# Running gate/up of all units, then down of all, in the last two passes of a two-layer kernel

## The chip, the cores and the metric

The kernel runs on one core of a Trainium2 chip. The metric is the device time of one execution in microseconds. Three runs of the kernel before took 908.52, 910.92 and 909.13 us; their median is 909.13 us.

## The reference, cut to what matters

Two blocks, A and B, are applied twice to an array `x` of 2048 rows and 576 columns. A is a gated long convolution: a four-tap shift of `k`, times `v`, a causal convolution over the 2048 rows by FFT, then a gate by the layer-normed `x`. B is a gated feed-forward block with 4608 hidden columns.

```python
def _B_ref(x, w_gate, w_up, w_down):
    return (_gelu(x @ w_gate) * (x @ w_up)) @ w_down

x = A_q
x = x + _A_ref(_layernorm(x, axis=-1), A_k, A_v, A_shift_k, A_ssm_k, A_ssm_D)
x = x + _B_ref(_layernorm(x, axis=-1), B_w_gate, B_w_up, B_w_down)
x = x + _A_ref(_layernorm(x, axis=-1), A_k, A_v, A_shift_k, A_ssm_k, A_ssm_D)
x = x + _B_ref(_layernorm(x, axis=-1), B_w_gate, B_w_up, B_w_down)
```

Both uses of A have the same `k`, `v` and filter, so the convolution's result `y` is computed once and used by both layers. Both uses of B have the same three weight matrices.

## The kernel before, in words

**Units and passes.** The 2048 rows are cut into four chunks of 512. A unit is one layer of one chunk, and there are eight, in the order (0,0), (0,1), (1,0), (1,1), (0,2), (0,3), (1,2), (1,3) as (layer, chunk). Units are grouped into passes, `passes = [[0], [1, 2], [3, 4], [5, 6], [7]]`. The weights are streamed from HBM in each pass, and the units of one pass share what is loaded. So pass 3 is units 5 and 6 (layer 0 of chunk 3, layer 1 of chunk 2), and pass 4 is unit 7 alone (layer 1 of chunk 3). Unit 6 needs unit 4's result, and unit 7 needs unit 5's.

**Phases and visits.** The 4608 hidden columns are 36 tiles of 128, cut into `NP = 3` phases of `FP = 12` tiles. A visit is one unit in one phase. It has two stretches on TensorE. In the first, gate/up (line 1758), each of 12 tiles takes nine pairs of matmuls; the two of a pair use one half of the array's rows each and run side by side, gate in one half and up in the other. ScalarE makes the GELU of gate (line 1767), VectorE multiplies it with up into the tile `hT` (line 1768). In the second stretch, down (line 1792), four row tiles of 128 rows are each summed over the 12 hidden tiles in PSUM, in two halves of 288 columns. VectorE then adds the sum into `x_c` (line 1831, or line 1823 in layer 0's last phase, or line 1814 into the output tile `ob` in layer 1's last phase). So a unit's down product is gathered in three parts, one in each phase.

**Memory.** `hT` has one buffer of 12 KB per partition and `wd` (the down weights, six hidden tiles each) has three of 6.9 KB. `wgu` (gate and up weights, four hidden tiles each) has three buffers. The convolution keeps its own pools (`c_cst` to `c_kv`, lines 107 to 116) until the end of the kernel, although its last matmul is in pass 2. PSUM has three accumulators that gate/up and down share.

**What sets the order.** The instructions of every engine are written out in program order by a planner that keeps estimated clocks of TensorE, VectorE and ScalarE (`t.pe`, `t.dve`, `t.act`) and, through `fill`, puts work for the next unit between the matmuls of the current one. Weight loads get a due time by `when_due`, but `weights` holds one back only while the layer norm of unit 1 or unit 5 is being turned (`turning`, lines 1387 and 1723); at all other times it issues everything in the list at once, in the order of the due times:

```python
near = turns_near() and left_to_turn()
if near and due[0][0] > t.pe + HOLD:
    break
_, _, load, n = due.pop(0)
load(n)
```

**From one unit to the next.** After the last down of unit 4, its four row tiles go through the second layer's gate and two rounds of statistics, on VectorE, ScalarE and GpSimd, to a normed tile `xn` (line 1302). Two DMA transposes for each row tile then write it, turned, into `xnT` (`spread`, line 1335). Gate/up of unit 6 reads all 512 columns of `xnT` in each matmul, so it cannot begin before the last of the eight transposes has landed. Unit 5's visit lies in between. Loads of `wd` (line 1202), of `wgu` (lines 1192 to 1194) and these transposes are all issued by SyncE, in program order, on one queue. Stores of the output and of the convolution go through GpSimd's queue.

Of the kernel before, what the change touches and what calls it, by code (L numbers as in the profile page):

```python
# [16 lines left out]
ALU = mybir.AluOpType  # L17
F32 = mybir.dt.float32
BF16 = mybir.dt.bfloat16
# [8 lines left out]
HW = 288  # L28
EPS = 1e-5
NP = 3  # L30
FG = 4
NEVER = 1e9

# [53 lines left out]
class Conv:  # L87
# [9 lines left out]
    def __init__(self, spare, tc, ctx, pace, A_k, A_v, A_shift_k, A_ssm_k, A_ssm_D, ident, psp, cpsp, ypool):  # L97
# [9 lines left out]
        pool = lambda name, bufs: ctx.enter_context(tc.tile_pool(name=name, bufs=bufs))  # L107
        self.cst = pool("c_cst", 1)
        self.krp = pool("c_kr", 3)
        self.hrp = pool("c_hr", N_HR)  # L110
# [391 lines left out]
    def step(self, m, kv=None, loaded=False):  # L502
# [630 lines left out]
def ssm_geglu_kernel(ctx, tc, A_q, A_k, A_v, A_shift_k, A_ssm_k, A_ssm_D, B_x, B_w_gate, B_w_up,  # L1133
# [61 lines left out]
        wgu[n] = w  # L1195

    def load_wd(n):
        if n >= NWB * 2:
            return
        r0 = (n % (NP * 2)) * WT * P  # L1200
        d = dpool.tile([P, WT, D], BF16, tag="wd", name="wd")
        nc.sync.dma_start(out=d[:], in_=B_w_down[r0:r0 + WT * P, :].rearrange("(ft p) d -> p ft d", p=P))
        wd[n] = d
# [240 lines left out]
    with tc.manual_schedule():  # L1444
# [150 lines left out]
        hpool = pool("hT", 1)  # L1595
        dpool = pool("wd", 3)
        for n in range(3):
            load_wd(n)

# [90 lines left out]
        for m in range(2, NCH):  # L1690
            conv.filt(m)
            conv.step(m)

        xn_done[0] = RT
        at_start = {(0, 1): [("es", 1)], (0, 2): [("prep", 1)], (1, 0): [("x", 2)], (2, 1): [("es", 2)],
                    (3, 0): [("prep", 4)], (3, 1): [("x", 3)], (4, 1): [("es", 3)], (4, 2): [("prep", 5)]}
# [10 lines left out]
        conv.clear = lambda: xn_at[1] + LANDED if xn_done.get(1, 0) >= RT else NEVER  # L1707
        visits = []
        for pi, us in enumerate(passes):
            visits += [(pi * NP + ph, ph, ui, k == 0, k == len(us) - 1)  # L1710
                       for ph in range(NP) for k, ui in enumerate(us)]
        for wb, ph, ui, first, final in visits:
            layer, c = units[ui]
            while xn_done.get(ui, 0) < RT:
                if not run_vq(t.pe + 3.0):
                    conv.run_loads()
                    run_aq(t.pe + 3.0)
                    conv.run_v(t.pe + 1.5)
                    conv.run_p()
                    t.pe += 0.2  # L1720
                spreads()
            if (ui, ph) == (4, 2):
                turning.append(5)
            for kind, n in at_start.get((ui, ph), []):
# [12 lines left out]
            end = ph == NP - 1  # L1737
            hT = hpool.tile([P, FP, CH], BF16, tag="hT", name="hT")
            free = deque([0.0] * 3)
            if wb == 0:  # L1740
                first_half(hT)
# [9 lines left out]
            for fi in range(FP if wb else 0):  # L1751
                n, gi = divmod(wb * FP + fi, FG)
                w = wgu[n]
                pair = psp.tile([P, 2, 512], F32, tag="pr", name="gu")
                for k in range(NKC):
                    b = blk_of[k]
                    for s, r0 in ((0, 0), (1, HK)):
                        nc.tensor.matmul(pair[:, s, :], lhsT=w[r0:r0 + HK, k, gi * P:(gi + 1) * P],  # L1758
                                         rhs=xnT[r0:r0 + HK, b, :], start=(k == 0), stop=(k == NKC - 1))
                t.pe = max(t.pe, free.popleft()) + C_GU  # L1760
                if ui == 0 and (fi % 2 and rounded or fi % 2 == 0 and conv.left > 0):
                    rounded = True
                    free.append(hidden(hT[:, fi - fi % 2:fi - fi % 2 + 2, :], pair, fi % 2, 1))
                else:
                    rounded = False
                    ga = work.tile([P, CH], F32, tag="ga", name="ga")
                    nc.scalar.activation(out=ga[:], in_=pair[:, 0, :], func=ACT.Gelu_apprx_tanh)  # L1767
                    nc.vector.tensor_tensor(out=hT[:, fi, :], in0=ga[:], in1=pair[:, 1, :], op=ALU.mult)  # L1768
                    free.append(t.on_dve(C_HT, t.on_act(C_GELU, t.pe + 0.15) + 0.15) + 0.1)
                if conv.borrowed:  # L1770
                    free.popleft()
                    free.append(conv.borrowed)
                    conv.borrowed = None
                if gi == FG - 1 and final:
                    when_due(t.pe + (FP - FG) * C_GU + 12.0, load_wgu, n + 3)
# [4 lines left out]
            if ui == 0 and end:  # L1780
                unit0.clear()
            conv.window = t.pe + RT * FP * C_DN - SPARE if wb < NWB - 1 else -1.0
            for j in range(RT):
                acc = psp.tile([P, 2, 512], F32, tag="pr", name="dn")
                last = wb == NWB - 1 and j == RT - 1
                part = [acc, psp.tile([P, 2, 512], F32, tag="pr", name="dn") if last else acc]
                xa = x_c[c][:, j, :]
                xh = xa.rearrange("p (h d) -> p h d", h=2)

                def down(fi, h):  # L1790
                    at = AT0[j] if ui == 0 else j
                    nc.tensor.matmul(part[h][:, h, 0:HW], lhsT=hT[:, fi, at * P:(at + 1) * P],  # L1792
                                     rhs=wd[2 * wb + fi // WT][:, fi % WT, h * HW:(h + 1) * HW],
                                     start=(fi == 0), stop=(fi == FP - 1))
                if last:
                    dst = out2[c * CH:(c + 1) * CH, :].rearrange("(p j) d -> p j d", j=RT)[:, j, :]
                    for h in range(2):
                        for fi in range(FP):
                            down(fi, h)
                        ob = work.tile([P, D], BF16, tag="ob", name="ob")  # L1800
                        nc.vector.tensor_tensor(out=ob[:, 0:HW], in0=xh[:, h, :], in1=part[h][:, h, 0:HW], op=ALU.add)
                        nc.sync.dma_start(out=dst[:, h * HW:(h + 1) * HW], in_=ob[:, 0:HW])
                    break
                for fi in range(FP):
                    for h in range(2):
                        down(fi, h)
                    t.pe += C_DN
                    if fi < FP - 1:
                        if fi == FP // 2 and hurry():
                            conv.run_p(True)  # L1810
                        fill(t.pe + (HURRY if hurry() else 1.5), True, conv.left > 0)
                if layer == 1 and end:
                    ob = work.tile([P, D], BF16, tag="ob", name="ob")
                    nc.vector.tensor_tensor(out=ob[:].rearrange("p (h d) -> p h d", h=2), in0=xh,  # L1814
                                            in1=acc[:, :, 0:HW], op=ALU.add)
                    dst = out2[c * CH:(c + 1) * CH, :].rearrange("(p j) d -> p j d", j=RT)[:, j, :]
                    if wb == NWB - 1:
                        nc.sync.dma_start(out=dst, in_=ob[:])
                    else:
                        conv.store(dst, ob, t.pe + 0.2 + C_EVD + LAG)  # L1820
                elif end:
                    v = g_sum(c, j)
                    nc.vector.scalar_tensor_tensor(out=xh, in0=acc[:, :, 0:HW], scalar=1.0, in1=xh, op0=ALU.mult,  # L1823
                                                   op1=ALU.add, accum_out=v["s"][:])
                    mean_after(v, t.pe + 0.2 + C_EVD + LAG)
                    square_task(lambda xa=xa: xa, v)
                elif wb == 0 and "mean" in gvars[0][j]:
                    nc.vector.scalar_tensor_tensor(out=xh, in0=acc[:, :, 0:HW], scalar=gvars[0][j]["mean"], in1=xh,
                                                   op0=ALU.add, op1=ALU.add)
                else:  # L1830
                    nc.vector.tensor_tensor(out=xh, in0=xh, in1=acc[:, :, 0:HW], op=ALU.add)  # L1831
                t.on_dve(C_EVD, t.pe + 0.2)
                if layer == 0 and end:
                    vq.extend(prep(units.index((1, c)), j))
        conv.flush(NEVER)


# [48 lines left out]
```

## Time and profile before

| | us |
|---|---|
| median of three runs (908.52 to 910.92) | 909.13 |
| span of the profiled execution | 908.5 |
| TensorE matmul busy | 902.1 (99%) |
| VectorE busy | 575.9 (63%) |
| ScalarE busy | 328.8 (36%) |
| GpSimd busy | 158.2 (17%) |
| gate/up matmuls, line 1758 (4968) | 540.7 |
| down matmuls, line 1792 (2304) | 292.1 |
| `x_c` adds, line 1831 (62) | 46.6 |

The page gives no time of the profiled execution apart from its span of 908.5 us, which is 0.6 us under the median of the runs and 0.02 us from the fastest of them. In the views, a row of the timeline merges like instructions that follow each other on one engine: start, length, engine, line, tiles, and how many. The letter q behind an engine marks its queue, where DMAs are issued. `gu` is gate/up's accumulator, `dn` down's.

### The profile page before, as it was taken

To read this page: it belongs to the slowest core of one execution; us is meant where nothing else is said; L and a number is where in the kernel's file an instruction comes from. 1 tells how busy PE (TensorE), PEld (TensorE's weight loads), DVE (VectorE), ACT (ScalarE), POOL (GpSimd) and SP (SyncE) were. 2 spreads that over 40 slices of the span, in tenths; PEclk is the share of its full clock that TensorE was granted. 3 is DMA by queue.
4 is the path that set the end of the run, shared out by engine and by line. 5 is a ranking of instruction groups with operands and counts; after the bars stand their busy time and mean duration, and the time that the engine had idled before them with its cause. 6 is when DMAs were issued, how large, how long until landed. Compare 5 with 4: busy or idle time off the path is not lost.

```text
span 908.5 us, 19157 instructions
## 1 busy us (share of the span) xinstructions
PE 902.1 (99%) x8133; PEld 524.7 (58%) x8133; DVE 575.9 (63%) x984; ACT 328.8 (36%) x616; POOL 158.2 (17%) x336
## 2 busy tenths in 40 slices
PE   9999999999999999999999999999999999999998
PEld 6875646556465465564654655645646646556555
DVE  7989976688888884787898855443333335332332
ACT  6765455523223254443125133551121125321221
POOL 3333315120223031420104002310000003100000
PEclk9999999999999999999999999999999999999999
DMA  9999997666629319785915601961520721966620
GB/s 260 301 298 295 221 226 139 193 190 147 198 92 266 95 27 172 210 142 131 273 55 133 169 3 42 187 137 41 123 73 15 143 80 27 190 162 172 142 55 27
DMA packets 132075, 132.90 MB, mean 146 GB/s; under 512 B 46139, under 2 KB 123670, under 8 KB 131990
## 3 DMA queue, kind: packets, MB, share of 16 engines
q1 hardware_dynamic: 121728, 94.65, 46.2%
q0 software_dynamic: 10208, 37.02, 13.0%
q8 instruction: 63, 1.03, 0.5%
q14 instruction: 22, 0.18, 0.1%
q10 hardware_dynamic: 54, 0.01, 0.0%
HBM read 108.36 MB, written 12.39 MB: 133 GB/s over the span
## 4 chain that ended last, share of the span: by engine, by line
PE 97%; DVE 2%; DMA 1%; SPq 0%; issue 0%; ACT 0%; DVEq 0%
PE gu L1758 59%; PE dn L1792 31%; PE gu L1677 3%; PE cps L282 1%; PE ps L415 1%; DMA hn<-in_A_ssm_k_dram 1%; PE cps L415 1%; PE ps L282 0%; DVE yb L362 0%; PE cps L823 0%; DVE prod L359 0%; DVE h L233 0%; DVE prod L361 0%; PE xps L1477 0%; DVE v L990 0%; PE pt L963 0%
## 5 line engine op out<-in xcount | busy, mean ns | idle before, releaser
L1758 PE MATMUL gu<-xnT,wgu 64*128 64x512 bf16 x4968 | 540.7, 376 | 0.0
L1758 PEld LDWEIGHTS <-wgu 64*128 64x128 bf16 x4968 | 239.7, 94 | 294.4 <-issue 5.9
L1767 ACT ACTIVATE ga<-gu 128x512 f32<-128x512 f32 x258 | 153.9, 596 | 451.1 <-PE gu L1758 442.7
L1768 DVE TENSOR_TENSOR hT<-ga,gu 128x512 bf16<-128x512 f32 x258 | 177.0, 686 | 200.0 <-ACT ga L1767 198.4
L1792 PE MATMUL dn<-wd,hT 128*128 128x288 bf16 x2304 | 292.1, 286 | 0.0
L1792 PEld LDWEIGHTS <-hT 128*128 128x128 bf16 x2304 | 223.5, 98 | 65.6 <-issue 9.5
L1831 DVE TENSOR_TENSOR x_c<-x_c,dn 128x576 f32<-128x576 f32 x62 | 46.6, 752 | 55.3 <-PE dn L1792 54.9
L1230 POOL TENSOR_SCALAR nm<-s 128x1 f32<-128x1 f32 x56 | 20.4, 365 | 270.5 <-DVE x_c L1823 210.8
L1238 ACT ACTIVATE junk<-x_c,nm 128x576 bf16<-128x576 f32 x48 | 36.9, 768 | 28.0 <-POOL nm L1230 25.9
L560 POOL DMA_DIRECT2D hr<-Hd x32 | 17.4, 545 | 117.7 <-DVE prod L361 117.1
L1246 POOL TENSOR_TENSOR rstd<-ve,neghalf_t 128x1 f32<-128x1 f32 x58 | 36.8, 635 | 4.8
L1302 ACT ACTIVATE xn<-x_c,nb,rstd 128x576 bf16<-128x576 f32 (+1 forms) x48 | 28.6, 644 | 5.9 <-POOL nb L1250 5.7
L1245 POOL TENSOR_SCALAR ve<-ss 128x1 f32<-128x1 f32 x58 | 21.8, 375 | 45.9 <-ACT junk L1238 45.8
L1814 DVE TENSOR_TENSOR ob<-x_c,dn 128x576 bf16<-128x576 f32 x15 | 11.3, 754 | 29.0 <-PE dn L1792 29.0
L285 ACT COPY eo<-cps 128x576 f32<-128x576 f32 x29 | 18.6, 643 | 27.3 <-PE cps L282 24.1
L1656 ACT ACTIVATE ga<-gu 128x512 bf16<-128x512 f32 x26 | 15.5, 598 | 30.5 <-PE gu L1758 25.9
L1677 PE MATMUL gu<-xnT,wgu 64*128 64x256 bf16 x432 | 24.8, 269 | 0.3 <-ACT xnT L1484 0.3
L1677 PEld LDWEIGHTS <-wgu 64*128 64x128 bf16 x432 | 21.4, 94 | 3.2 <-issue 1.2
L362 DVE TENSOR_TENSOR prod<-prod 128x576 bf16<-128x576 bf16 x48 | 22.0, 458 | 1.7
L430 POOL DMA_DIRECT2D out_dram<-ob x12 | 6.7, 562 | 91.6 <-DVE ob L1814 91.6
L245 DVE SCALAR_TENSOR_TENSOR eo<-eo 128x576 f32<-128x576 f32 x22 | 16.3, 753 | 5.8 <-ACT eo L285 5.8
L1280 DVE SCALAR_TENSOR_TENSOR x_c<-g_t,rstd,x_c 128x576 f32<-128x576 f32 x16 | 13.0, 814 | 8.6 <-POOL rstd L1246 8.6
(182 smaller groups left out, 591.3 us busy)
## 6 DMA issues: line engine op xcount, KB each, us to landing
wgu<-in_B_w_gate_dram SPq DMA_DIRECT2D x45, 576.0 KB, 5.6
wd<-in_B_w_down_dram SPq DMA_DIRECT2D x30, 864.0 KB, 7.1
wgu<-in_B_w_up_dram SPq DMA_DIRECT2D x45, 512.0 KB, 7.6
hr<-Hd POOLq DMA_DIRECT2D x32, 288.0 KB, 5.0
kr<-Kd POOLq DMA_DIRECT2D x24, 288.0 KB, 5.3
Kd<-kc POOLq DMA_DIRECT2D x12, 288.0 KB, 6.2
k<-in_A_k_dram POOLq DMA_DIRECT2D x3, 1008.0 KB, 12.0
wgu<-in_B_w_up_dram SPq DMA_DIRECT2D x45, 64.0 KB, 7.7
```

Source lines behind the costliest of these rows:

```text
L362: nc.vector.tensor_tensor(out=dst, in0=pr[:, 0, :], in1=pr[:, 1, :], op=ALU.subtract if part == 0 else ALU.add)
L1230: nc.gpsimd.tensor_scalar(out=v["nm"][:], in0=v["s"][:], scalar1=-1.0 / D, scalar2=None, op0=ALU.mult)
L1238: nc.scalar.activation(out=junk[:], in_=get_x(), func=ACT.Square, bias=v["nm"][:, 0:1], accum_out=v["ss"][:])
L1245: nc.gpsimd.tensor_scalar(out=ve[:], in0=v["ss"][:], scalar1=1.0 / D, scalar2=EPS, op0=ALU.mult, op1=ALU.add)
L1246: nc.gpsimd.tensor_tensor(out=v["rstd"][:], in0=ve[:], in1=neghalf_t[:, 0:1], op=ALU.pow)
L1302: nc.scalar.activation(out=xn[:, lo:hi], in_=x_c[c][:, j, 0:hi - lo], func=ACT.Identity, scale=v["rstd"][:, 0:1], bias=v["nb"][:, 0:1])
L1677: nc.tensor.matmul(pair[:, s, e * 256:(e + 1) * 256], lhsT=w[r0:r0 + HK, k, gi * P:(gi + 1) * P], rhs=xnT[r0:r0 + HK, blk_of[k], tok], sta ...
L1758: nc.tensor.matmul(pair[:, s, :], lhsT=w[r0:r0 + HK, k, gi * P:(gi + 1) * P], rhs=xnT[r0:r0 + HK, b, :], start=(k == 0), stop=(k == NKC - 1))
L1767: nc.scalar.activation(out=ga[:], in_=pair[:, 0, :], func=ACT.Gelu_apprx_tanh)
L1768: nc.vector.tensor_tensor(out=hT[:, fi, :], in0=ga[:], in1=pair[:, 1, :], op=ALU.mult)
L1792: nc.tensor.matmul(part[h][:, h, 0:HW], lhsT=hT[:, fi, at * P:(at + 1) * P], rhs=wd[2 * wb + fi // WT][:, fi % WT, h * HW:(h + 1) * HW], s ...
L1831: nc.vector.tensor_tensor(out=xh, in0=xh, in1=acc[:, :, 0:HW], op=ALU.add)
```

## The change

Passes 0 to 2 stay as they were. When pass 3 begins, the pools of `hT` and `wd` and all pools of the convolution are closed, and two new ones are opened in their place: `hT2` with six buffers and `wd2` with six. In pass 3 the visits now run gate/up alone: unit 5 and 6 in phase 0, in phase 1, in phase 2. After the last of these, `down_rows` runs down for unit 5 and then for unit 6, each row tile summed over all 36 hidden tiles at once. In pass 4, gate/up of unit 7 runs through its three phases and then its down. A pass's six `wd` loads are put on the list together when its first visit begins, with a due time of 60 us later; before, two were put on the list at each phase. In phase 2 of pass 2, the load of the first `wd` tile of pass 3 is left out.

```diff
+WHOLE = 3
...
+    def close(self):
+
+        assert not (self.U or self.V or self.L or self.Pq or self.late)
+        self.flush(NEVER)
+        self.pools.close()
...
+        def down_rows(wb, ph, ui):
...
+            hs = hidden_of.pop(ui)
+            nf = FP * len(hs)
+            for j in range(RT):
...
+                def down(fi, h):
+                    at = AT0[j] if ui == 0 else j
+                    wk, hT = hs[fi // FP]
+                    f = fi % FP
+                    nc.tensor.matmul(part[h][:, h, 0:HW], lhsT=hT[:, f, at * P:(at + 1) * P],
+                                     rhs=wd[2 * wk + f // WT][:, f % WT, h * HW:(h + 1) * HW],
+                                     start=(fi == 0), stop=(fi == nf - 1))
...
-            visits += [(pi * NP + ph, ph, ui, k == 0, k == len(us) - 1)
-                       for ph in range(NP) for k, ui in enumerate(us)]
-        for wb, ph, ui, first, final in visits:
+            each = [(pi * NP + ph, ph, ui, k == 0, k == len(us) - 1)
+                    for ph in range(NP) for k, ui in enumerate(us)]
+            if pi < WHOLE:
+                visits += [v + (v[:2],) for v in each]
+            else:
+                visits += [v + (None,) for v in each[:-len(us)]]
+                last = each[-len(us):]
+                visits += [v + (None,) for v in last[:-1]] + [last[-1] + (us,)]
+        for wb, ph, ui, first, final, downs in visits:
...
+            if (pi, ph, first) == (WHOLE, 0, True):
+                first_pools.close()
+                conv.close()
+                hpool = pool("hT2", NP * 2)
+                dpool = pool("wd2", NP * 2)
...
-            if first and wb > 0:
+            if pi >= WHOLE:
+                if first and ph == 0:
+                    for n in range(NP * 2):
+                        when_due(t.pe + 60.0, load_wd, 2 * wb + n)
+            elif first and wb > 0:
                 when_due(t.pe + FP * C_GU, load_wd, 2 * wb + 1)
-                when_due(t.pe + FP * C_GU + 35.0, load_wd, 2 * wb + 2)
+                if wb < WHOLE * NP - 1:
+                    when_due(t.pe + FP * C_GU + 35.0, load_wd, 2 * wb + 2)
             weights()
...
+            if downs is None:
+                continue
+            if pi < WHOLE:
+                down_rows(wb, ph, ui)
+            else:
+                for u in downs:
+                    down_rows(wb, ph, u)
```

More of the change, by code (lines that the diff above doesn't have):

```diff
@@ L106, in __init__ @@
         D = self.D
-        pool = lambda name, bufs: ctx.enter_context(tc.tile_pool(name=name, bufs=bufs))
+        self.pools = ctx.enter_context(ExitStack())
+        pool = lambda name, bufs: self.pools.enter_context(tc.tile_pool(name=name, bufs=bufs))
         self.cst = pool("c_cst", 1)
@@ L1197, in load_wd @@
     def load_wd(n):
-        if n >= NWB * 2:
-            return
         r0 = (n % (NP * 2)) * WT * P
@@ L1593, in ssm_geglu_kernel @@
         conv.begin(head, tables)
-        hpool = pool("hT", 1)
-        dpool = pool("wd", 3)
+        first_pools = ctx.enter_context(ExitStack())
+        hpool = first_pools.enter_context(tc.tile_pool(name="hT", bufs=1))
+        dpool = first_pools.enter_context(tc.tile_pool(name="wd", bufs=3))
         for n in range(3):
@@ L1692, in ssm_geglu_kernel @@
             conv.step(m)
+        hidden_of = {}
+        def down_rows(wb, ph, ui):
+            layer, c = units[ui]
+            end = ph == NP - 1
+            if ui == 0 and end:
+                unit0.clear()
+            conv.window = t.pe + RT * FP * C_DN - SPARE if wb < WHOLE * NP else -1.0
+            hs = hidden_of.pop(ui)
+            nf = FP * len(hs)
+            for j in range(RT):
+                acc = psp.tile([P, 2, 512], F32, tag="pr", name="dn")
+                last = ui == NU - 1 and end and j == RT - 1
+                part = [acc, psp.tile([P, 2, 512], F32, tag="pr", name="dn") if last else acc]
+                xa = x_c[c][:, j, :]
+                xh = xa.rearrange("p (h d) -> p h d", h=2)
+                def down(fi, h):
[5 more added lines that the diff above has]
+                                     start=(fi == 0), stop=(fi == nf - 1))
+                if last:
+                    dst = out2[c * CH:(c + 1) * CH, :].rearrange("(p j) d -> p j d", j=RT)[:, j, :]
+                    for h in range(2):
+                        for fi in range(nf):
+                            down(fi, h)
+                        ob = work.tile([P, D], BF16, tag="ob", name="ob")
+                        nc.vector.tensor_tensor(out=ob[:, 0:HW], in0=xh[:, h, :], in1=part[h][:, h, 0:HW], op=ALU.add)
+                        nc.sync.dma_start(out=dst[:, h * HW:(h + 1) * HW], in_=ob[:, 0:HW])
+                    break
+                for fi in range(nf):
+                    for h in range(2):
+                        down(fi, h)
+                    t.pe += C_DN
+                    if fi < nf - 1:
+                        if fi == FP // 2 and hurry():
+                            conv.run_p(True)
+                        fill(t.pe + (HURRY if hurry() else 1.5), True, conv.left > 0)
+                if layer == 1 and end:
+                    ob = work.tile([P, D], BF16, tag="ob", name="ob")
+                    nc.vector.tensor_tensor(out=ob[:].rearrange("p (h d) -> p h d", h=2), in0=xh,
+                                            in1=acc[:, :, 0:HW], op=ALU.add)
+                    dst = out2[c * CH:(c + 1) * CH, :].rearrange("(p j) d -> p j d", j=RT)[:, j, :]
+                    if ui == NU - 1:
+                        nc.sync.dma_start(out=dst, in_=ob[:])
+                    else:
+                        conv.store(dst, ob, t.pe + 0.2 + C_EVD + LAG)
+                elif end:
+                    v = g_sum(c, j)
+                    nc.vector.scalar_tensor_tensor(out=xh, in0=acc[:, :, 0:HW], scalar=1.0, in1=xh, op0=ALU.mult,
+                                                   op1=ALU.add, accum_out=v["s"][:])
+                    mean_after(v, t.pe + 0.2 + C_EVD + LAG)
+                    square_task(lambda xa=xa: xa, v)
+                elif wb == 0 and "mean" in gvars[0][j]:
+                    nc.vector.scalar_tensor_tensor(out=xh, in0=acc[:, :, 0:HW], scalar=gvars[0][j]["mean"], in1=xh,
+                                                   op0=ALU.add, op1=ALU.add)
+                else:
+                    nc.vector.tensor_tensor(out=xh, in0=xh, in1=acc[:, :, 0:HW], op=ALU.add)
+                t.on_dve(C_EVD, t.pe + 0.2)
+                if layer == 0 and end:
+                    vq.extend(prep(units.index((1, c)), j))
@@ L1774, in ssm_geglu_kernel @@
                 if gi == FG - 1 and final:
-                    when_due(t.pe + (FP - FG) * C_GU + 12.0, load_wgu, n + 3)
+                    when_due(t.pe + (FP - FG) * C_GU + (12.0 if downs else 0.0), load_wgu, n + 3)
                 fill(t.pe + lead(FP - 1 - fi if ui == 0 else FP), now(), conv.left > 0)
@@ L1779, in ssm_geglu_kernel @@
                 run_made()
[L1780 to L1834, printed above, removed]
@@ L1835, in ssm_geglu_kernel @@
+            if downs is None:
+                continue
+            if pi < WHOLE:
+                down_rows(wb, ph, ui)
+            else:
+                for u in downs:
+                    down_rows(wb, ph, u)
         conv.flush(NEVER)
```

4 lines of the change are left out of this document (3 added, 1 removed).

## The prediction

> **What bounds the kernel now.** I read the page's head first, then the chain that ended last, then TensorE's timeline over the last two passes.
>
> ```profile
> span 908.5 us, 19157 instructions
> ...
> PE 902.1 (99%) x8133; PEld 524.7 (58%) x8133; DVE 575.9 (63%) x984; ACT 328.8 (36%) x616; POOL 158.2 (17%) x336
> ...
> PE 97%; DVE 2%; DMA 1%; SPq 0%; issue 0%; ACT 0%; DVEq 0%
> ```
>
> ```profile
> 575.41 11.93 PE L1792 MATMUL dn<-wd,hT 128*128 128x288 bf16 x96
> 587.28 23.48 PE L1758 MATMUL gu<-xnT,wgu 64*128 64x512 bf16 x216
> 610.70 11.94 PE L1792 MATMUL dn<-wd,hT 128*128 128x288 bf16 x96
> 622.56 23.48 PE L1758 MATMUL gu<-xnT,wgu 64*128 64x512 bf16 x216
> ```
>
> The reader is to see that TensorE is the bound and has no hole: each row starts where the one above ends. Pass 2 ends with unit 4's down (575.41), pass 3 begins with unit 5's visit (587.28), and unit 6 begins at 622.56. The change leaves every matmul in place, so it can win only what the switches between gate/up and down cost, and it can lose wherever TensorE has to wait.
>
> **The switches.** The chain gives the pitch, because its pieces run from start to start. Its rows for gate/up and for down, in stretches of several lengths:
>
> ```profile
> 408.52 2.05 PE gu L1758 x18
> ...
> 410.92 21.47 PE gu L1758 x198
> ...
> 587.35 23.42 PE gu L1758 x216
> ```
>
> ```profile
> 359.76 1.23 PE dn L1792 x10
> ...
> 365.88 5.63 PE dn L1792 x46
> ...
> 575.48 11.87 PE dn L1792 x96
> ```
>
> Gate/up: (21.47 - 2.05) / 180 = 0.1079 us for one matmul, so 216 are 23.30; a visit takes 23.42, and the 0.12 left over is the switch. Down: (5.63 - 1.23) / 36 = 0.1222, so 96 are 11.73; a visit takes 11.87, and 0.14 is left. An alternation thus costs up to 0.26 us; the rows have two decimals, and I take 0.21. The last two passes have nine gate/up and nine down stretches; after the change they have two and two. Seven alternations go: 7 x 0.21 = **1.5 us won** (at most 1.8, at least 1.2).
>
> **Adds that go.** Down's parts of phases 0 and 1 were added into `x_c` by VectorE:
>
> ```profile
> L1831 DVE TENSOR_TENSOR x_c<-x_c,dn 128x576 f32<-128x576 f32 x24 | 18.1, 754 | 49.7 <-PE dn L1792 49.7
> ```
>
> All 24 of this stretch (from 587.3 us on) go, 18.1 us of VectorE. I cost that at nothing: each add runs while TensorE fills another of the three accumulators. An accumulator is now held for 36 x 2 x 0.1222 = 8.8 us instead of 2.9, which gives the add more room. The last gate/up product, on which down waited next, now belongs to the last of 36 terms.
>
> **The step that I expect to lose: unit 6 begins earlier, and its input lands later.** Between unit 4's down and unit 6's gate/up lay unit 5's whole visit, 622.56 - 587.28 = 35.3 us. After the change only unit 5's gate/up lies there: unit 6 is due at 587.28 + 23.30 = **610.6**. What it needs are eight transposes on SyncE's queue:
>
> ```profile
> 580.79 0.59 SPq L1192 DMA_DIRECT2D wgu<-in_B_w_gate_dram  x1
> ...
> 586.44 2.52 SPq L1335 DMA_TRANSPOSE xnT<-xn  x2
> 589.06 2.55 SPq L1202 DMA_DIRECT2D wd<-in_B_w_down_dram  x2
> 591.71 13.66 SPq L1335 DMA_TRANSPOSE xnT<-xn  x6
> 630.54 0.64 SPq L1192 DMA_DIRECT2D wgu<-in_B_w_gate_dram  x1
> ```
>
> ```profile
> 601.65 1.19 ACT L1302 ACTIVATE xn<-x_c,nb,rstd 128x576 bf16<-128x576 f32 x2
> ```
>
> ```profile
> L1335 SPq DMA_TRANSPOSE xnT<-xn x8: 1200/1264/4107, 586.4 to 604.1; - x8
> ...
> DMA to landing us min/median/max: 2.4/5.5/8.6
> ```
>
> The reader is to see the order on the queue: two transposes, two `wd` loads, six transposes. The last transpose starts at 604.1, right behind its `xn` (ready at 602.8), and lands 2.4 us later, at 606.6. That alone would be 4 us early for 610.6. But the due time of 60 us holds nothing back here, since neither unit 1 nor unit 5 is being turned then. So the list is emptied at the start of the visit, and all six `wd` loads stand where two stood, ahead of the six transposes. What the DMA engines did in that stretch (columns: stretch, TensorE, its weight loads, VectorE, ScalarE, GpSimd, clock, DMA share, GB/s):
>
> ```profile
> 589.00:594.50 5.50, 5.50 (x54) 2.52 (x52) 3.37 (x8) 3.71 (x7) 2.97 (x8) 1.00 1.23 142
> 594.50:599.00 4.50, 4.50 (x46) 2.01 (x44) 2.60 (x5) 3.80 (x9) 1.51 (x6) 1.00 1.08 376
> 599.00:601.50 2.50, 2.50 (x26) 1.11 (x24) 0.69 (x1) 0.94 (x2) 0.67 (x2) 1.00 1.59 268
> 601.50:604.00 2.50, 2.50 (x26) 1.16 (x24) 1.02 (x2) 1.93 (x4) 0.00 (x0) 1.00 0.03 3
> 607.00:610.70 3.70, 3.70 (x37) 1.50 (x33) 1.38 (x2) 1.11 (x2) 0.00 (x0) 1.00 0.00 0
> ```
>
> The loads run from 594.5 at 376 GB/s, behind the gate/up weights of 580.79, then the transposes at 268 GB/s. A load is 864 KB, 0.885 MB: 2.35 us. Six take 14.1 us, to 608.6 (two ended at 599.2). Three row tiles to be turned are 3 x 128 x (640 + 512) x 2 bytes = 0.885 MB: 3.3 us at 268 GB/s, to 611.9. Add 1.2 us to land (the last transpose: 2.4 from its start, less 1.2 for its issue): **613.1**. TensorE waits 613.1 - 610.6 = **2.5 us lost**. Bounds: nothing, if the transposes are not delayed; 7.0 us, if they are issued only when the loads have drained (third rival). I take 2.5, because DMA work was already queued there, and it drains at a measured rate.
>
> The Trainium skill ("DMA: Bandwidth & Descriptors", Specifications) gives about 358 GB/s as a core's limit from HBM. By that the six loads would take an estimated 14.8 us, the wait would be 3.2 and the time 0.7 us more than mine. The row at 376 GB/s speaks against it, so the row decides.
>
> **Edits that I cost at nothing, and what covers them.**
> - The new pools: the convolution's buffers add up to 85.6 KB per partition, the old `hT` and `wd` to 33.0; the new pools need 73.7 + 41.5 = 115.2 of these 118.7. The first load there waits for unit 4's down, which ends at 575.41 + 11.93 = 587.3, and its place on the queue is 589.06. If it waited longer, the wait above would grow by as much.
> - The six loads of pass 4 reach the queue when unit 6's down frees them, one each 12 x 0.1222 = 1.5 us, the last at the end of pass 3. Behind them stands the `wgu` load that unit 7 needs after 23.3 us. Even if all began at that moment they would take 14.1 us, and a gate/up load 8.2 (630.54 to landing at 638.7: its third part is issued at 631.91 and takes 6.8). That is 22.3: free, but by 1 us.
>
> ```profile
> 631.91 0.62 SPq L1194 DMA_DIRECT2D wgu<-in_B_w_up_dram  x1
> ```
>
> ```profile
> DMA to landing us min/median/max: 5.6/6.2/6.8
> ```
>
> - `wgu` loads within a pass: a buffer is freed after 7.8 us of gate/up and needed 15.5 us later, where down gave 11.9 more. They need 8.2.
> - Unit 7's input: between unit 5's down and unit 7 lay unit 6's visit of phase 2, 35.3 us; now unit 6's whole down lies there, 288 x 0.1222 = 35.2. Nothing else is on the queue then.
> - The `wd` load left out of pass 2, and the small GpSimd steps that closing issues early: neither was waited for.
> - The end: the last row tile still runs one half behind the other and then stores, and the first half gets 4.4 us to store instead of 1.5.
>
> **Sum**: -1.5 + 2.5 = +1.0 on the profiled span of 908.5, so 909.5. The median of the runs is 0.6 above that span: **910.1 us**, +0.1%. I call a difference of less than 0.3% (2.7 us) no change, which is about what a measurement of this kernel can tell.
>
> **The rivals.**
> 1. *No wait.* The transposes land by 610.6, since the six loads wait elsewhere or run faster. Only the switches count: 909.1 - 1.5 = **907.6**. Against it: the loads are on the same queue, ahead of them, and the two transposes issued at 586.44 took up to 8.6 us behind loads. The Trainium skill ("DMA: Bandwidth & Descriptors", Queues, rings and completion order) says that each DMA engine takes descriptors in ring order; this trace agrees, with those 8.6 us against 2.4 on an empty queue.
> 2. *The second burst.* Pass 4's six loads delay `wgu`: 1 us of slack, and by gate/up's speed each later group has 7.8 us for 1.2 MB. A delay of 3 us would give about **913**. For it: DMA at 142 GB/s in the first stretch of the table above. Against it: five of six loads can start before pass 4 does.
> 3. *The issue blocks (the other side).* A full queue holds SyncE itself: one of the eight transposes took 4.1 us to issue instead of 1.2. If the first of the six gets out only when the loads have drained, at 608.6, and four issues take 5.19 us as below, six take 7.8, plus 1.2 to land: 617.6, a wait of 7.0 and +5.5: **914.6**. It decides from a wait of 4.2 us on, a landing after 614.8.
>
> ```profile
> 563.63 5.19 SPq L1335 DMA_TRANSPOSE xnT<-xn  x4
> ```
>
> A wait of 7 us would be new to this kernel: TensorE's longest is 1.2 us, and the granted clock reads 1.00 in all rows above.
>
> ```profile
> PE cps L895 <- DVE below L872: 1.2, 1, 1.2
> ```
>
> The Trainium skill ("TensorE: Matmul & The Clock Gate", Part 1) says that an idle window of about 3.4 us halves the clock until some 3.4 us of work have passed; on the third rival that would put an estimated 1.7 us. No run here shows it.
>
> **How the numbers follow.** Forecast, a wait of 1 to 4 us: 0.52, all of it within 0.3%; its own range is 908.6 to 911.6. No wait: 0.10, of which 0.04 faster by over 0.3%, should the switches cost twice what I read. Second burst: 0.05, slower. Blocked issue, or a wait of over 4.2 us by a slower drain: 0.33, slower. Faster 0.04, same 0.58, slower 0.38. The range goes from the no-wait case, 907.5, to the blocked one, 914.6.
>
> **What would show it.** In TensorE's timeline of the changed kernel: gate/up rows without down between them; one hole of 1 to 4 us before unit 6 near 610.6, released by a DMA into `xnT`; six `wd` issues between the first two transposes and the next six; gate/up of 432 matmuls in 46.6 us. A hole at unit 7 or inside pass 4 would prove the second burst; transposes issued only after 608 the third rival. The prediction is wrong if there is no hole, if it exceeds 4.2 us, or if a switch costs other than 0.2 us.

## The result, and the profile after

The changed kernel takes 910.55 us (median of ten runs, 909.48 to 911.79), the kernel before 908.38 us (ten runs). The ratio is 1.0019, with a 95% interval of 1.0011 to 1.0027: 0.2% slower, which is inside what I had called no change, and on the side that I had forecast.

TensorE's timeline of the changed kernel, from pass 3 on:

```profile
585.95 23.48 PE L1848 MATMUL gu<-xnT,wgu 64*128 64x512 bf16 x216
611.05 0.39 PE L1848 MATMUL gu<-xnT,wgu 64*128 64x512 bf16 x2 [1.61 <-DMA xnT<-xn]
612.32 118.20 PE L1848 MATMUL gu<-xnT,wgu 64*128 64x512 bf16 x1078 [0.88 <-DMA xnT<-xn]
730.45 70.73 PE L1723 MATMUL dn<-wd,hT 128*128 128x288 bf16 x576
801.12 70.10 PE L1848 MATMUL gu<-xnT,wgu 64*128 64x512 bf16 x648
871.15 35.45 PE L1723 MATMUL dn<-wd,hT 128*128 128x288 bf16 x288
```

The reader is to see the alternations gone, and two holes before unit 6 that end with a transpose into `xnT`. There are two because the first pair of matmuls needs only the first of a row tile's two transposes and the next pair needs the second; so unit 6 begins one pair before the last of the eight transposes has landed. After that there is no wait to the end.

SyncE's queue, and the landing of the loads and of the transposes (columns of the last two rows: issue time in ns as minimum, median and maximum, first and last start; below each, the time to landing):

```profile
585.12 2.52 SPq L1341 DMA_TRANSPOSE xnT<-xn  x2
587.95 10.35 SPq L1208 DMA_DIRECT2D wd<-in_B_w_down_dram  x6
598.41 12.67 SPq L1341 DMA_TRANSPOSE xnT<-xn  x6
```

```profile
L1208 SPq DMA_DIRECT2D wd<-in_B_w_down_dram x6: 388/2074/2426, 588.0 to 596.1; - x6
...
DMA to landing us min/median/max: 7.2/10.2/11.8
```

```profile
L1341 SPq DMA_TRANSPOSE xnT<-xn x8: 1215/1265/5493, 585.1 to 609.8; - x8
...
DMA to landing us min/median/max: 2.5/5.1/10.1
```

The last transpose starts at 609.8 and lands 2.5 us later, at 612.3; TensorE resumes at 612.32. The first of the six was held in its issue for 5.5 us, from 598.4 to 603.9; the other five followed on SyncE one behind another:

```profile
L1341 SPq DMA_TRANSPOSE xnT<-xn x5: 1221/1265/1623, 604.0 to 609.8; - x5
```

And stretches of the same run (TensorE, its weight loads, VectorE, ScalarE, GpSimd, granted clock, DMA share, GB/s):

```profile
592.50:605.50 13.00, 13.00 (x124) 5.88 (x122) 6.06 (x10) 7.93 (x15) 2.19 (x7) 1.00 1.08 386
...
604.00:606.00 2.00, 2.00 (x22) 0.88 (x18) 0.69 (x1) 0.66 (x2) 0.00 (x0) 1.00 1.08 383
606.00:608.00 2.00, 2.00 (x22) 0.90 (x20) 0.69 (x1) 0.65 (x2) 0.00 (x0) 1.00 1.35 106
608.00:610.00 2.00, 1.44 (x14) 0.47 (x10) 0.69 (x1) 0.66 (x2) 0.00 (x0) 1.00 1.02 216
610.00:612.40 2.40, 0.47 (x4) 0.25 (x6) 0.69 (x1) 0.07 (x1) 0.00 (x0) 1.00 0.49 105
...
613.42:616.83 3.41, 3.41 (x20) 1.50 (x18) 0.69 (x1) 0.60 (x1) 0.00 (x0) 0.50 0.02 5
617.00:640.00 23.00, 23.00 (x216) 12.09 (x214) 7.68 (x12) 7.17 (x12) 0.00 (x0) 1.00 0.52 116
```

The loads keep the engines at 383 to 386 GB/s until about 606. From there on the stretches shown move 105 to 216 GB/s on average, and the last transpose lands as fast as it did before the change (2.5 us against 2.4), so it was no longer behind other work: what set its landing was its issue, the last of five behind the one that got out at 603.9.

Right behind the hole the granted clock is 0.50 for 3.41 us, and then 1.00 again. In every stretch of the profile of before that is shown above it was 1.00.

**The balance.** Spans of single runs differ in the start of the kernel: pass 3 begins at 587.28 in the profile of before and at 585.95 here, with the same program up to there. So I measure from pass 3's first matmul to the end of the last one. Before: 892.96 + 11.93 - 587.28 = 317.61 us. After: 871.15 + 35.45 - 585.95 = 320.65 us. That is 3.04 us more. The terms are -1.49 us for the seven alternations (measured below, in kernels without a hole), 2.83 us of standing (what TensorE lost around the two rows of 1.61 and 0.88 us), and 3.41 / 2 = 1.70 us of half clock. The standing is worked out from the same kernels: there gate/up of pass 3 takes 139.96 us from its start to down's, here 730.45 - 585.95 = 144.50; of the 4.54 more, 1.70 are the clock's.

The drop of the clock does not come in every run. In seven of the ten runs the mean granted clock was 0.998, which is what 3.41 us at half speed make of 910 us; they took 910.51 to 911.79 us, and the profiled run is the slowest of them. In two it was 1.000, and they took 909.48 and 909.72. One run of 910.20 us reads 0.999 and cannot be told: runs of the kernel before, which has no such hole, read 0.999 too.

### The profile page after: what moved, and what is told of

The parts are those of the page before. It is cut to its first block, busy times and chain, and to the rows that moved or that the text cites. A ratio compares the mean times of both kernels' runs of the same rounds, so it can differ in the third digit from the quotient of the medians.

```text
span 910.0 us, 19126 instructions
## 1 busy us (share of the span) xinstructions
PE 901.8 (99%) x8133; PEld 534.5 (59%) x8133; DVE 558.4 (61%) x960; ACT 329.7 (36%) x616; POOL 157.2 (17%) x336
## 3 DMA queue, kind: packets, MB, share of 16 engines
q8 instruction: 63, 1.03, 0.5%
## 4 chain that ended last, share of the span: by engine, by line
PE 97%; DVE 2%; SPq 0%; ACT 0%; DMA 0%; issue 0%; DVEq 0%
PE gu L1848 59%; PE dn L1723 31%; PE gu L1684 3%; PE cps L284 1%; PE ps L417 1%; PE cps L417 1%; PE ps L284 0%; DVE yb L364 0%; SPq L1341 0%; DVE prod L361 0%; PE cps L831 0%; DVE h L235 0%; DVE prod L363 0%; DMA xnT<-xn 0%; PE cps L903 0%; PE xps L1483 0%
## 5 line engine op out<-in xcount | busy, mean ns | idle before, releaser
L1848 PEld LDWEIGHTS <-wgu 64*128 64x128 bf16 x4968 | 249.3, 94 | 289.8 <-issue 7.3
L1745 DVE TENSOR_TENSOR ob<-x_c,dn 128x576 bf16<-128x576 f32 x15 | 11.3, 754 | 67.6 <-PE dn L1723 67.6
L562 POOL DMA_DIRECT2D hr<-Hd x32 | 17.5, 547 | 117.7 <-DVE prod L363 117.0
L1762 DVE TENSOR_TENSOR x_c<-x_c,dn 128x576 f32<-128x576 f32 x38 | 28.6, 751 | 5.5 <-PE dn L1723 5.2
L1754 DVE SCALAR_TENSOR_TENSOR x_c<-dn,x_c 128x576 f32<-128x576 f32 x16 | 12.1, 754 | 26.0 <-PE dn L1723 26.0
L1684 PEld LDWEIGHTS <-wgu 64*128 64x128 bf16 x432 | 21.4, 94 | 3.2 <-issue 1.2
```

The lines of the kernel that those rows point to most:

```text
L1684: nc.tensor.matmul(pair[:, s, e * 256:(e + 1) * 256], lhsT=w[r0:r0 + HK, k, gi * P:(gi + 1) * P], rhs=xnT[r0:r0 + HK, blk_of[k], tok], sta ...
```

## The experiments

All edits are to the changed kernel. The table gives, for each profiled run, the time from pass 3's first matmul to the last matmul's end, less the 317.61 us of before, and the ratio of the timed runs to the kernel before on the same chip.

| kernel | passes 3 and 4, us | ratio, 95% interval |
|---|---|---|
| the changed kernel | +3.04 | 1.0019 (1.0011 to 1.0027) |
| loads held back | -1.49 | 0.9987 (0.9978 to 0.9996) |
| five loads ahead | -0.67 | 0.9989 (0.9980 to 0.9998) |
| six and 1.03 MB more ahead | +6.87 | 1.0070 (1.0056 to 1.0083) |
| six loads by GpSimd | +1.57 | 1.0014 (1.0005 to 1.0023) |
| hole filled, 24 matmuls | +1.66 | 1.0014 (1.0006 to 1.0023) |
| hole half filled, 12 matmuls | +1.58 | 1.0018 (1.0009 to 1.0027) |
| pass 4 alone, six loads at once | +0.73 | 1.0011 (1.0003 to 1.0020) |
| pass 4 alone, two loads a phase | -0.42 | 0.9997 (0.9988 to 1.0005) |
| two loads a phase | -1.49 | 0.9979 (0.9970 to 0.9987) |
| held back, pass 4 loads nothing | -1.49 | 0.9976 (0.9966 to 0.9985) |

### Are the loads ahead of the transposes the cause?

The planner is told that unit 6 is being turned, so that it holds loads back as it does for units 1 and 5:

```diff
                 if first and ph == 0:
+                    if pi == WHOLE:
+                        turning.append(6)
                     for n in range(NP * 2):
                         when_due(t.pe + 60.0, load_wd, 2 * wb + n)
```

> The changed kernel, with the six down-weight loads of pass 3 held until unit 6's transposes are on the queue. Theory (the loads ahead of the transposes make the hole, and the hole drops the clock): the transposes land near 606 on the old time line, the hole of 1.6 + 0.9 us before unit 6 and the half clock of 3.4 us behind it both go, and only the seven switches are left as a difference to the kernel before: -1.5 us, about 906.9, ratio 0.9983. Rival (the cover of 23.3 us instead of 35.3 is too short by itself, whoever stands on the queue): the hole stays at 2 us or more, ratio 1.001 to 1.003. Second rival (closing the pools or the longer sums cost something outside the hole): no hole, but no gain either, ratio 0.9995 or more.

Measured: 907.23 us against 908.51, ratio 0.9987. TensorE's timeline:

```profile
585.96 140.03 PE L1850 MATMUL gu<-xnT,wgu 64*128 64x512 bf16 x1296
725.92 70.73 PE L1723 MATMUL dn<-wd,hT 128*128 128x288 bf16 x576
```

And its transposes:

```profile
L1341 SPq DMA_TRANSPOSE xnT<-xn x8: 1200/1240/1265, 585.1 to 602.8; - x8
```

All 1296 gate/up matmuls of pass 3 run without a hole, in 725.92 - 585.96 = 139.96 us, and no transpose takes over 1.3 us to issue. So a cover of 23.3 us is long enough, and the loss came with the loads. The ratio stayed 0.04% above the number expected; the time in the two passes, -1.49 us, is the one expected.

With one load fewer ahead:

```diff
-                    for n in range(NP * 2):
+                    for n in range(NP * 2 - (pi == WHOLE)):
                         when_due(t.pe + 60.0, load_wd, 2 * wb + n)
+                elif (ui, ph) == (6, 0):
+                    when_due(t.pe + 60.0, load_wd, 2 * wb + 5)
```

> The changed kernel with five loads ahead of the transposes instead of six; the sixth is issued when unit 6 begins. Theory: a load takes 2.3 us of the queue (0.885 MB at 388 GB/s), so the hole of 2.5 to 2.8 us shrinks to about 0.5; that is too short to drop the clock, so 1.7 us more come back: about -1.0 us against the kernel before, 907.4, ratio 0.999. Rival (the hole is set by the issue of the transposes themselves, 1.3 us each on SyncE): the hole shrinks by the same 2.2 us if they wait for ring space, but stays above 1.5 us if they are issued one by one after the loads.

Measured: 907.66 us, ratio 0.9989. One hole is left:

```profile
610.03 116.51 PE L1850 MATMUL gu<-xnT,wgu 64*128 64x512 bf16 x1078 [0.65 <-DMA xnT<-xn]
```

In the balance the standing is 1.49 - 0.67 = 0.8 us, 2.0 us less than with six; the clock stayed at 1.00. The same 1078 matmuls took 118.20 us in the changed kernel and take 116.51 here, so the half clock cost 1.69 us there. This run does not tell the theory from transposes that wait for room on the queue: the rival gave the same 2.2 us for that.

In the other direction, 1.03 MB more go ahead, into buffers that nothing reads:

```diff
+                    if pi == WHOLE:
+                        weights()
+                        for rows, room in ((3, pad), (RT, xbp)):
+                            d = room.tile([P, rows, D], BF16, ...)
+                            nc.sync.dma_start(out=d[:], in_=B_w_down[0:rows * P, :]...)
```

> The changed kernel with 1.03 MB more (three and four hidden tiles of down weights, into room that nothing reads) loaded behind the six loads and ahead of the six transposes. Theory (the transposes wait for the bytes ahead of them, 388 GB/s): they land 1.03 / 0.388 = 2.7 us later, the waits before unit 6 are 2.5 + 2.7 = 5.2 us, and the clock drops as before for one stretch of 3.4 us: 2.7 us more than the changed kernel in its runs with the drop, so about +4.6 us on the kernel before, 913.1, ratio 1.0050. Rival (the transposes wait for their issue on SyncE, not for bytes): the hole grows by less than 1.5 us. Second rival (the half clock grows with the hole): half clock for two stretches, ratio 1.007.

Measured: 914.84 us against 908.61, ratio 1.0070. TensorE's timeline, and the stretch of half clock:

```profile
614.18 0.61 PE L1854 MATMUL gu<-xnT,wgu 64*128 64x512 bf16 x2 [4.71 <-DMA xnT<-xn]
615.50 118.88 PE L1854 MATMUL gu<-xnT,wgu 64*128 64x512 bf16 x1078 [0.71 <-DMA xnT<-xn]
```

```profile
613.53:620.30 6.77, 5.41 (x26) 1.88 (x28) 0.53 (x1) 0.60 (x1) 0.00 (x0) 0.50 0.11 23
```

The waits grew from 2.49 to 5.42 us, 2.9 for the 2.7 that the bytes account for. So the wait follows the bytes ahead on the queue, over three sizes; that the bytes act through an issue held until the queue has room fits this too. The ratio is the second rival's and not the 1.0050 of the theory: half speed lasted 6.8 us here, twice the stretch of 3.4. The part of it before 615.50 fell into the hole and cost little; behind it gate/up took 118.88 us against 116.51 without a drop, 2.4 us more.

### Is it the place on the queue, or the engines' time?

Pass 3's six loads are issued by GpSimd:

```diff
                     for n in range(NP * 2):
-                        when_due(t.pe + 60.0, load_wd, 2 * wb + n)
+                        if pi == WHOLE:
+                            load_wd(2 * wb + n, nc.gpsimd)
+                        else:
+                            when_due(t.pe + 60.0, load_wd, 2 * wb + n)
```

> The changed kernel with pass 3's six loads issued by GpSimd instead of SyncE, at the same place: the same bytes over the same DMA engines, but not on the transposes' queue. Theory (the transposes wait because they stand behind the loads on one queue): sharing the engines with the loads, they land before the loads are done; no hole, or one under 0.5 us, no drop of the clock, and about -1.3 us, 907.2, ratio 0.9986. Rival (the DMA engines' time is what is short, whichever queue): the last transpose still lands at about 26 us after the start of pass 3, with the hole at 2 us or more and ratio 1.001 to 1.002. Should GpSimd's issue of the loads hold up the small steps of unit 6's norm that run on GpSimd, a hole appears whose wait is traced to these and not to the transfer.

Measured: 909.77 us, ratio 1.0014. My theory missed; the ratio is the rival's, and the hole by GpSimd's issue came as well. TensorE's timeline, the DMA queues from 598 to 602 us (q0 carries GpSimd's loads, q1 the transposes), and GpSimd's issue with the steps of unit 6's norm behind it:

```profile
597.22 13.77 PE L1851 MATMUL gu<-xnT,wgu 64*128 64x512 bf16 x126 [1.79 <-DVE hT L1861]
611.66 116.98 PE L1851 MATMUL gu<-xnT,wgu 64*128 64x512 bf16 x1080 [0.66 <-issue]
```

```profile
DMA packets 696, 1.55 MB, mean 389 GB/s; under 512 B 378, under 2 KB 378, under 8 KB 696
...
q0 software_dynamic: 350, 1.47, 96.7%
q1 hardware_dynamic: 346, 0.09, 9.8%
```

```profile
588.94 5.04 POOL L1208 DMA_DIRECT2D wd<-in_B_w_down_dram  x6
...
594.89 0.82 DVE L1286 SCALAR_TENSOR_TENSOR x_c<-g_t,rstd,x_c 128x576 f32<-128x576 f32 x1 [2.32 <-POOL rstd L1252]
...
601.87 1.19 ACT L1308 ACTIVATE xn<-x_c,nb,rstd 128x576 bf16<-128x576 f32 x2
```

On two queues the engines took about one packet from each in turn in these 4 us, 350 against 346. But a packet of the transposes holds 0.09 MB / 346 = 0.26 KB and one of the loads 1.47 MB / 350 = 4.2 KB, so the transposes got 0.09 of 1.55 MB; the one issued at 599.7 took 11.3 us to land, and unit 6 began 26.1 us after the start of pass 3, against 26.4 in the changed kernel. The Trainium skill ("DMA: Bandwidth & Descriptors", Queues, rings and completion order) says that an engine takes turns between queues packet by packet; these counts agree, if the profile's packets are the same thing. The first hole is a new one: GpSimd spent 5.0 us on issuing the loads, the small steps of unit 6's norm waited behind that on GpSimd, and VectorE's products behind those. The clock stayed at 1.00, with two holes of 1.8 and 0.7 us. The same hold-up made the last normed tile ready later, 601.87 + 1.19 - 585.54 = 17.5 us after the start of pass 3 against 15.6 in the changed kernel. So this run shows that the shared engines slow the transposes on a queue of their own; how much earlier they would land without GpSimd's hold-up it does not show. What a queue of its own would give with large packets was not tried.

### What does the clock cost?

The hole is filled with idle matmuls into an accumulator that nothing reads:

```diff
+            if (ui, ph) == (6, 0):
+                idle = cpsp.tile([P, 2, 512], F32, tag="cps", name="cps")
+                for _ in range(24):
+                    nc.tensor.matmul(idle[:, 0, 0:HW], lhsT=ident[:], rhs=hidden_of[5][0][1][:, 0, 0:HW], ...)
```

> The changed kernel with 24 idle matmuls of 128 x 288 (24 x 0.122 = 2.9 us) between unit 5's and unit 6's first gate/up; all else as it was, the six loads ahead too. Theory (the hole costs twice: once as time, once as 3.4 us of half clock behind it): the transposes land as late as before, so TensorE still begins unit 6 at the same time, but busy, and the clock stays at 1.00: 1.7 us less than the changed kernel's profiled run, +1.3 us on the kernel before, ratio 1.0014, and no spread into two groups of runs. Rival (the dropped clock is an accident of the run and not of the hole): half clock somewhere all the same, and the time equals the changed kernel's, ratio 1.0019 or more.

Measured: 909.87 us (909.60 to 910.60), ratio 1.0014:

```profile
608.82 3.12 PE L1832 MATMUL cps<-hT,ident 128*128 128x288 bf16 x24
611.86 116.72 PE L1852 MATMUL gu<-xnT,wgu 64*128 64x512 bf16 x1080
```

```profile
612.00:616.00 4.00, 4.00 (x40) 1.78 (x38) 0.69 (x1) 0.63 (x2) 0.00 (x0) 1.00 0.02 4
```

Unit 6 begins no earlier, 26.5 us after the start of pass 3 against 26.4 with the hole, but the clock stays at 1.00 in all eleven runs, and 1.4 us come back in the two passes. That it is not the whole 1.7 fits the filling being a little long: the last transpose landed at 609.0 + 2.5 = 611.5, and the idle matmuls ran on to 611.9.

With 12 instead of 24:

> The changed kernel with 12 idle matmuls (1.5 us) before unit 6, half of those that filled the hole. Theory: the transposes land at the same time, so unit 6 begins at the same time; TensorE stands still for about 1.3 us instead of 2.5. If the clock drops only after more than some 2 us of standing still, it stays at 1.00 in all runs, and the time is that of the filled kernel, ratio 1.0014. Rival (any hole over 1 us can drop it): half clock in some or all runs, ratio up to 1.0030.

Measured: 909.81 us, ratio 1.0018, and the clock was 1.000 in all ten runs:

```profile
610.70 0.39 PE L1852 MATMUL gu<-xnT,wgu 64*128 64x512 bf16 x2 [0.28 <-DMA xnT<-xn]
611.96 116.51 PE L1852 MATMUL gu<-xnT,wgu 64*128 64x512 bf16 x1078 [0.87 <-DMA xnT<-xn]
```

Waits of 0.28 + 0.87 = 1.15 us did not drop the clock. The ratio is above the expected one, but its interval holds it, and in the two passes the two filled kernels differ by 0.1 us. The runs still spread from 909.11 to 911.75 us with the clock at 1.000, so the time of a single run does not tell whether the clock dropped.

### Pass 4 alone

`WHOLE = 4` leaves pass 3 as it was before.

> The change in pass 4 alone (WHOLE = 4): pass 3 as in the kernel before, unit 7 whole, its six loads at the start of pass 4. Theory: two of the seven alternations go, 2 x 0.21 = 0.4 us less than the kernel before, 907.9, ratio 0.9995, no hole anywhere, since unit 7's transposes are on the queue before the loads. Rival (the second burst of six loads delays gate/up weights in pass 4): a hole at unit 7's fourth group or later, and a time above the kernel before.

Measured: 909.68 us, ratio 1.0011: the theory missed, and the rival held. The wait, and SyncE's queue at the start of pass 4:

```profile
PE gu L1848 <- DMA wgu<-in_B_w_up_dram: 0.8, 1, 0.8
```

```profile
797.72 9.35 SPq L1208 DMA_DIRECT2D wd<-in_B_w_down_dram  x6
807.17 2.54 SPq L1200 DMA_DIRECT2D wgu<-in_B_w_gate_dram  x1
```

Here the old buffers are given up only when pass 4 begins: SyncE waits 9.2 us for pass 3's last down before the first of the six loads, and unit 7's fourth group of gate/up weights comes 0.8 us late. In the changed kernel the six start at 793.9, as unit 6's down frees them, and nothing waits. Gate/up of pass 4 took 868.81 - 797.62 = 71.19 us here and 70.03 in the changed kernel: 1.2 us, of which the row shows 0.8.

With the loads spread:

```diff
-                if first and ph == 0:
-                    for n in range(NP * 2):
+                if first:
+                    for n in range(2):
                         when_due(t.pe + 60.0, load_wd, 2 * wb + n)
```

> The change in pass 4 alone, with its loads two at the start of each phase instead of six at the start of the pass. Theory (in the run with six, the burst held up the gate/up weights of unit 7's fourth group, 0.8 us and a switch of clock not seen): that wait goes, and only the two alternations are left: -0.4 us against the kernel before, ratio 0.9995, and 0.8 us less than with six at once. Rival (the wait there was not from the burst, or something else in the shorter form costs time): a time above the kernel before with no wait of TensorE in pass 4.

Measured: 908.24 us, ratio 0.9997, no wait in pass 4:

```profile
797.25 70.10 PE L1848 MATMUL gu<-xnT,wgu 64*128 64x512 bf16 x648
```

Two alternations fewer gave -0.42 us in the two passes, 0.21 each. One thing stays open: in both kernels with `WHOLE = 4` the time of a run is 2.1 us above its span, in all others 1.8, and no view shows what lies there.

### A version that beats both

The same spread with `WHOLE = 3`:

> The changed kernel with two down-weight loads at the start of each phase of passes 3 and 4, as before the change, instead of six at the start of the pass. Theory (the number of loads ahead of the transposes decides): with two ahead the last transpose lands where it did before the change, some 4 us before unit 6 needs it; no hole, no half clock, -1.5 us by the seven alternations, 907.1, ratio 0.9983 to 0.9988, the same as with all six held back. Rival (spread loads now meet the gate/up weights inside the passes, where no down stretch gives room): a wait of TensorE for wgu, and a time above that of the held loads.

Measured: 906.60 us against 908.69, ratio 0.9979 (0.9970 to 0.9987), below the expected range, of which the interval holds the lower part. The interval lies below 1, and below that of the changed kernel. There is no hole and no wait for `wgu`, so the rival did not happen:

```profile
585.31 140.03 PE L1848 MATMUL gu<-xnT,wgu 64*128 64x512 bf16 x1296
725.27 70.73 PE L1723 MATMUL dn<-wd,hT 128*128 128x288 bf16 x576
```

```profile
584.48 2.52 SPq L1341 DMA_TRANSPOSE xnT<-xn  x2
587.31 1.82 SPq L1208 DMA_DIRECT2D wd<-in_B_w_down_dram  x2
589.24 14.16 SPq L1341 DMA_TRANSPOSE xnT<-xn  x6
```

With the loads held back, and pass 4 reading the tiles that pass 3 left (`wd[2 * wb + n] = wd[2 * WHOLE * NP + n]` in place of its loads):

> The kernel with held loads, and pass 4 reads the six down-weight tiles that pass 3 left in their buffers instead of loading them again: 5.3 MB less traffic. Theory (pass 4's loads are hidden): no change against the held loads, ratio 0.9983 to 0.9990 against the kernel before. Rival (the second burst costs something in pass 4 that shows as no wait, or drives the spread of the runs): at least 0.5 us less than with the held loads.

Measured: 906.67 us, ratio 0.9976 (0.9966 to 0.9985), below the expected range, whose lower end the interval holds. In the two passes the kernels with held loads, with two loads a phase and with none in pass 4 take the same 316.12 us, so pass 4's loads were hidden. The median with held loads was 0.6 us higher, as the rival had it, but it was timed on another chip, and its extra time does not lie in these passes: in its profiled run pass 3 begins at 585.96, against 585.31 and 585.46, with the same program ahead of it. The three intervals overlap.

## Why the prediction was right, and where it was not

- **The switches.** Forecast 1.5 us for seven alternations, 0.21 each. Measured 1.49 for seven and 0.42 for two.
- **Unit 6's wait.** Forecast 2.5 us before unit 6, with six loads ahead of six transposes; measured 2.5 in the two rows and 2.8 as standing. The cause was right, as the held loads show; the size is near in part by luck, because two terms were off in opposite directions. From the start of pass 3, the loads were to be through at 608.6 - 587.28 = 21.3 us, and their bytes were through at about 606 - 585.95 = 20.1; the rate was 386 instead of 376 GB/s. From there the last transpose was to land 4.5 us later, with the transposes drained at 268 GB/s, and it landed 6.3 us later, because they left SyncE one at a time. The rate also goes against the 358 GB/s of the Trainium skill ("DMA: Bandwidth & Descriptors", Specifications) that I had weighed.
- **The third rival's mechanism was real, its size was not.** The end was set by issue on SyncE, as this rival had it. But one transpose took 5.5 us to issue behind the full queue and got out at 603.9, 18.0 us after the start of pass 3, and not when the loads had drained, for which the rival had 21.3. So the wait lay between no delay and its 7.0 us.
- **A reading of the prediction.** It gives up to 8.6 us to landing for the two transposes issued at 586.44. The 8.6 belong to the one issued at 591.7, behind the two `wd` loads; those two took 8.3 and 7.5. The argument is the same.
- **The second rival did not happen in the changed kernel**, with pass 4's gate/up in 801.12 + 70.03. It did in the kernel with `WHOLE = 4`, where the loads cannot start early.
- **The adds, the buffers, the weights within a pass, unit 7's input and the end** cost nothing, as forecast: there is no wait of TensorE after 612.32.
- **The step that failed: the clock.** I had put the half clock beside the third rival alone, and nothing of it on a wait of 2.5. It came on waits of 2.5 us, in seven of ten runs or eight, and cost 1.7 us in the profiled one. So +1.0 us by my sum was +3.0 in the profiled run, and +2.2 between the medians.
- **The base.** I had the profiled span 0.6 us below the median. A span is not the time of a run, though: the spans of the 33 runs of before beside the first experiments have a median of 906.7 us, and their times 908.5: 1.8 us lie outside a span, so the profile of before was a run of about 910.3 us and not near the fastest; its pass 3 begins 1.3 us later than in the changed kernel's profile. The difference that I forecast did not hang on it, but the forecast time did: that 910.1 lies so near the measured 910.55 is luck, since the base of 909.13 was 0.75 us too high and the clock was missing.

## What to carry to other kernels

When work between two dependent steps is taken away, count what stands ahead of the dependent transfer on its queue, in bytes, and the issues that follow one behind another, over the shorter cover; a due time in a planner is worth only what its condition lets through. Waits of 2.5 us on an otherwise dense TensorE cost 1.7 us more than themselves here, so price the clock with a wait. The gain of fewer switches here was small and exact, so a single misplaced group of loads was enough to turn its sign, and spreading the loads again kept it.

## What the runs showed of the hardware

- Behind waits of 2.5 us the clock was halved for 3.41 us in the profiled run, and the mean clock of six more runs of the ten, perhaps seven, fits that. Behind waits of 5.4 us it was halved for 6.77 us, and all four runs read 0.996. With the shorter waits all thirty runs read 1.000: 1.8 and 0.7 us with the loads on GpSimd, 1.15 with half the hole filled, 0.65 with one load fewer ahead. The Trainium skill ("TensorE: Matmul & The Clock Gate", Part 1) speaks of a window of about 3.4 us that runs freely; the two stretches agree with one and two such lengths. If that window is at work here, it need not be all idle, since less than a window of standing was enough; no run here shows the window itself.
- Issuing a DMA transpose held SyncE for 1.2 us at the least, and for 5.5 us behind six loads of 0.885 MB.
- DMA transposes that shared the engines with loads on another queue got one packet in two from 598 to 602 us, and with 0.26 KB a packet against 4.2 that is 6% of the bytes.
